# Hedgehog attention beside a SwiGLU block: Q and K logits taken relative to the last feature of each head

## The chip, the cores and the metric

The kernel runs on one core of one Trainium2 chip. The metric is the time of one execution on the device in microseconds (us); the kernel before takes 266.25 us, the median of three runs (266.11 to 266.27). The profile is one such execution (266.31 us), of which the trace shows 265.1 us from the first instruction to the last. The core has a matrix engine (PE, TensorE, with its weight loads shown apart as PEld), a vector engine (DVE), an activation engine (ACT), GpSimd (POOL), and a queue (SP) that issues most of the transfers. All of them run beside each other and wait for one another through semaphores.

## The reference

The input is normalised once (`xn`), and two branches work on it: a linear attention with 32 heads of 20 features, and a gated MLP. Their sum is added to `x`. Cut to what matters:

```python
# S = 2048 rows, D = 640, H = 32 heads, Dh = 20, F = 1536, all bf16
q, k, v = split_heads(xn @ wqkv)
pq = jnp.einsum("bhsd,hdf->bhsf", q, w_phi)          # logits, 20 per head
pk = jnp.einsum("bhsd,hdf->bhsf", k, w_phi)
phi_q = concat([softmax(pq), softmax(-pq)], axis=-1)  # 40 features per head
phi_k = concat([softmax(pk), softmax(-pk)], axis=-1)
kv  = jnp.einsum("bhsf,bhsd->bhfd", phi_k, v)
z   = jnp.einsum("bhsf->bhf", phi_k)
num = jnp.einsum("bhqf,bhfd->bhqd", phi_q, kv)
den = jnp.einsum("bhqf,bhf->bhq", phi_q, z)[..., None] + 1e-6
attn = merge_heads(num / den) @ wo
mlp  = (silu(xn @ w1) * (xn @ w3)) @ w2
out  = x + attn + mlp
```

## The kernel before

The per-head matrices `w_phi` are multiplied into the Q and K columns of `wqkv` once, at the start (`fold_mm`: the folding), so that one matmul gives the logits straight from `xn`. The folded K weights lie beside the V weights in `WVK`, the folded Q weights in `Wqp`.

```python
def fold_mm(which, dc, k):              # 5 calls for K (which=1), 5 for Q (which=0)
    ...                                 # 6 or so narrow matmuls into two PSUM banks
    dst = Wqp[:, dc, :] if which == 0 else WVK[:, dc, D:2 * D]
    evac(dst..., bank2(k, 320))         # 640 columns, PSUM -> bf16, on ACT or DVE

def k_exps(t, c):                       # t: one of 16 tiles of 128 rows
    o = ekt[:, t, :].rearrange("p (h s f) -> p h s f", s=2, f=DH)
    i = PS[:, c:c + D].rearrange("p (h f) -> p h f", f=DH)
    for sg in range(2):                 # exp(x) and exp(-x)
        act(o[:, :, sg, :], i, ACT.Exp, 1.0 if sg == 0 else -1.0)

def k_features(t, k):                   # tiles 0 to 3 (their V was made before)
    for q, lo, hi in ((0, 0, 512), (1, 512, D)):
        for i in range(DC):             # DC = 5 slices of the 640 inputs
            mm(bank(k + q, hi - lo), xnT[:, i, t * 128:(t + 1) * 128], WVK[:, i, D + lo:D + hi], ...)
    k_exps(t, 512 * k)

def vk_features(t, k):                  # tiles 4 to 15: V and K in one go
    for q, lo, hi in ((0, 0, 512), (1, 512, 1024), (2, 1024, 2 * D)):
        for i in range(DC):
            mm(bank(k + q, hi - lo), xnT[:, i, ...], WVK[:, i, lo:hi], ...)
    act(v2c[:, t, :, 1:61], ..., ACT.Copy)
    k_exps(t, 512 * k + D)

def q_features(t, k):
    for q, lo, hi in ((0, 0, 18), (1, 18, 32)):        # heads
        n = DH * (hi - lo)                              # 360 and 280 columns
        for i in range(DC):
            mm(bank(k + q, n), xnT[:, i, ...], Wqp[:, i, DH * lo:DH * hi], ...)
        ...                                             # exp(x), exp(-x) on ACT into eqt

def normalise(e, c, n):                 # softmax's division, the same for Q and K
    tensor_reduce (DVE): sum over the 20 features of each of the 64 (66) groups
    reciprocal (DVE)
    tensor_tensor x2 (POOL): e = e * reciprocal, two halves of a tile
```

The K features of all 16 tiles are multiplied with V in `kv_sum`. A tile of Q features goes through a transposing transfer (`EqT`) and then `q_tok` multiplies it with the result of `kv_sum`; the quotient is transposed again into `oT`. The MLP is 48 units of ten 128x512 matmuls (`mlp`), which stand in no order with the attention, and the output matmuls end the kernel.

No engine has a hand-written order. A planner in the kernel holds a list of streams (norms, folding, attention, queries, MLP units, outputs and so on), estimates when each next piece could start, and puts the earliest one next; what comes out is one fixed list of instructions for each engine. MLP units thereby fill the places where the attention has to wait. `PACE0` and `PACE` say how many MLP units are to lie between two tiles of queries.

```python
def paced(t):
    left = NB * FC - 2 - pace[0]
    return PACE0 * t if t < 4 else PACE0 * 4 + min(PACE, (left - PACE0 * 4) / 12) * (t - 4)
```

Of the kernel before, what the change touches and what calls it, by code (L numbers as in the profile page):

```python
# [3 lines left out]
ACT = mybir.ActivationFunctionType  # L4
ALU = mybir.AluOpType
# [4 lines left out]
D = 640  # L10
H = 32
DH = 20
F = 1536
T = S // 128
DC = D // 128
FC = F // 128
NB = S // 512
# [10 lines left out]
def heads_of_chunk(c):  # L28
    return (128 * c) // DH, (128 * c + 127) // DH

# [215 lines left out]
def bass_parallel_sum__linear_kernel_hedgehog__glu_gated_swiglu__prompt_kernel(  # L246
# [11 lines left out]
    bf = DT.bfloat16  # L258
# [2 lines left out]
    LEAD = 5  # L261
    AHEAD = 0
    PACE = 2.6
    PACE0 = 2.6
    f32 = DT.float32
    P = _Program(nc)

# [5 lines left out]
    def region(size):  # L273
        o = top[0]
        top[0] = o + (size + 31) // 32 * 32
        assert top[0] <= arena_size, top[0]
        return a0 + o

    def new(name, shape, dtype, offset=None):
        size = mybir.dt.size(dtype)  # L280
        for n in shape[1:]:
            size *= n
        return P.sbuf(name, shape, dtype, region(size) if offset is None else offset)

    ident = new("ident", [128, 128], bf)
    GM = new("GM", [128, DC, H], bf)
    phi_s = new("phi_s", [128, DC, DH], bf)
    BDc = new("BDc", [128, DC, 8 * DH], bf)
    bst = new("bst", [128, T, 16], f32)
# [9 lines left out]
    xnT = new("xnT", [128, DC, S], bf)  # L299
    w1_s = new("w1_s", [128, DC, F], bf)  # L300
    w3_s = new("w3_s", [128, DC, F], bf)
    Wqp = new("Wqp", [128, DC, D], bf)
    th = new("th", [128, 3, 512], f32)
    RT = region(3072)
    t1 = new("t1", [128, 3, 512], bf, RT)
# [1 line left out]
    RR = region(4 * D * 2)  # L307
    xres = new("xres", [128, 4, D], bf, RR)
    xT1 = new("xT1", [128, DC, 512], bf, RR)

    RX = region(20480)
    x_tok = new("x_tok", [128, T, D], bf, RX)
    hT2 = new("hT2", [128, FC, 512], bf, RX)
    wo_s = new("wo_s", [128, DC, D], bf, RX + 12288)

    RKV = region(12800)
    WVK = new("WVK", [128, DC, 2 * D], bf, RKV)
    EqT0 = new("EqT0", [128, QC, 512], bf, RKV)
    xT2 = new("xT2", [128, DC, 512], bf, RKV)
    xT = {0: xT1, 1: xT1, 2: xT2}  # L320
# [6 lines left out]
    ekt = new("ekt", [128, T, 2 * D], bf, RE)  # L327
# [14 lines left out]
    eqt = new("eqt", [128, 3, QC * 128], bf, RW + 1408)  # L342
# [3 lines left out]
    PS = nc.alloc_psum_tensor("PS", [128, 8 * 512], f32)  # L346
# [3 lines left out]
    def bank(k, cols=512, off=0, rows=128):  # L350
        return PS[0:rows, k * 512 + off:k * 512 + off + cols]

    def bank2(k, cols):
        return PS[:, k * 512:(k + 2) * 512].rearrange("p (b c) -> p b c", c=512)[:, :, 0:cols]


    def mm(o, l, r, start, stop, shared=False, cost=None):
        n = free(r)
        P.op("PE", "matmul", [o], [l, r], (o, l, r),
             dict(start=start, stop=stop, skip_group_check=shared),  # L360
             cost=n / 2400 + 0.0027 if cost is None else cost)
# [11 lines left out]
    def act(o, i, f, scale=1.0):  # L373
        P.op("ACT", "activation", [o], [i], (o, i, f), dict(scale=scale),
             cost=0.17 + free(o) / 1200)

    def tt(eng, o, a, b, f, fast=1):
        c = 0.16 + free(o) / 960 / fast if eng == "DVE" else 0.2 + free(o) * 1.7 / 1000
        P.op(eng, "tensor_tensor", [o], [a, b], (o, a, b, f), cost=c)
# [5 lines left out]
    def copy(eng, o, i, fast=1):  # L385
        if eng == "ACT":
            act(o, i, ACT.Copy)
        else:
            P.op(eng, "tensor_copy", [o], [i], (o, i), cost=0.14 + free(o) / 960 / fast)

    def evac(o, i):

        a = P.free["ACT"] + 0.17 + free(o) / 1200
        d = P.free["DVE"] + 0.14 + free(o) / 960 / (2 if i.dtype == bf else 1)
        copy("ACT" if a <= d else "DVE", o, i, 2 if i.dtype == bf else 1)

    def memset(eng, o, v):
        P.op(eng, "memset", [o], [], (o, v), cost=0.15 + free(o) / 960)
# [138 lines left out]
    def fold_mm(which, dc, k):  # L537
        first = [True, True]
        for e in range(DC):
            h0, h1 = heads_of_chunk(e)  # L540
            lo, hi = DH * h0, DH * (h1 + 1)
            for q in range(2):
                a, b = max(lo, 320 * q), min(hi, 320 * q + 320)
                if a < b:
                    mm(bank(k + q, b - a, a - 320 * q), wqkT[:, which * DC + e, 128 * dc:128 * dc + 128],
                       BDc[:, e, a - lo:b - lo], first[q], e == DC - 1 or (q == 0 and e == 2), True)
                    first[q] = False
        dst = Wqp[:, dc, :] if which == 0 else WVK[:, dc, D:2 * D]
        evac(dst.rearrange("p (b c) -> p b c", c=320), bank2(k, 320))


    VH = (0, 300, D)

# [30 lines left out]

    def k_exps(t, c):
        o = ekt[:, t, :].rearrange("p (h s f) -> p h s f", s=2, f=DH)
        i = PS[:, c:c + D].rearrange("p (h f) -> p h f", f=DH)
        for sg in range(2):
            act(o[:, :, sg, :], i, ACT.Exp, 1.0 if sg == 0 else -1.0)

    def k_features(t, k):
        for q, lo, hi in ((0, 0, 512), (1, 512, D)):
            for i in range(DC):
                mm(bank(k + q, hi - lo), xnT[:, i, t * 128:(t + 1) * 128], WVK[:, i, D + lo:D + hi],
                   i == 0, i == DC - 1)
        k_exps(t, 512 * k)

    def vk_features(t, k):
        for q, lo, hi in ((0, 0, 512), (1, 512, 1024), (2, 1024, 2 * D)):
            for i in range(DC):  # L600
                mm(bank(k + q, hi - lo), xnT[:, i, t * 128:(t + 1) * 128], WVK[:, i, lo:hi], i == 0, i == DC - 1)
        act(v2c[:, t, :, 1:61], PS[:, 512 * k:512 * k + 660].rearrange("p (c n) -> p c n", n=60), ACT.Copy)
        k_exps(t, 512 * k + D)

    def q_features(t, k):
        if t < 3:
            e = eqt[:, t, :].rearrange("p (c r) -> p c r", r=128)
            memset("DVE", e[:, :, 120:128], 1.0)
            memset("DVE", e[:, QC - 1, 80:120], 1.0)
        for q, lo, hi in ((0, 0, 18), (1, 18, 32)):  # L610
            n = DH * (hi - lo)
            for i in range(DC):
                mm(bank(k + q, n), xnT[:, i, t * 128:(t + 1) * 128], Wqp[:, i, DH * lo:DH * hi],
                   i == 0, i == DC - 1)
            e = eqt[:, t % 3, :].rearrange("p (c r) -> p c r", r=128)[:, :, 0:120]
            e = e.rearrange("p c (h s f) -> p c h s f", s=2, f=DH)
            for sg in range(2):
                x = 1.0 if sg == 0 else -1.0
                if q == 0:
                    act(e[:, 0:6, :, sg, :], bank(k, n).rearrange("p (c h f) -> p c h f", h=3, f=DH), ACT.Exp, x)  # L620
                else:
                    act(e[:, 6:10, :, sg, :],
                        bank(k + 1, 240).rearrange("p (c h f) -> p c h f", h=3, f=DH), ACT.Exp, x)
                    act(e[:, 10, 0:2, sg, :], bank(k + 1, 40, 240).rearrange("p (h f) -> p h f", f=DH), ACT.Exp, x)

    nnorm, held = [0], {}

# [127 lines left out]
    def norms():  # L755
        yield lambda: (memset("DVE", zero[:], 0.0), memset("DVE", warm[:], 0.0), first_loads(), consts())
        yield lambda: act_sums(1)
        yield lambda: ln_stats(0, 1)
        yield lambda: act_mean(1)
        yield lambda: ln_apply(0, 0, 256)  # L760
        done["first"] = 1
        yield lambda: act_rstd(1)
        yield lambda: ln_apply(0, 256, D)
        done["first"], done["ln"] = 2, 1
        while done["t0"] < 2:
            yield None
        yield lambda: ln_sums(2, 0)
        yield lambda: ln_apply(1)
        done["ln"] = 2
        yield lambda: (ln_sums(2, 1), ln_rstd(2, 1))  # L770
        yield lambda: ln_sums(3, 0)
        yield lambda: ln_apply(2)
        done["ln"] = 3
        yield lambda: (ln_sums(3, 1), ln_rstd(3, 1))
        yield lambda: ln_apply(3)
        done["ln"] = 4
        yield block_diag
        todo = []
        for t in range(4, T + 2, 2):
            if t == T or t > done["k"] + LEAD or t == 12 and done["t"] < 8:  # L780
                for u in todo:
                    yield lambda u=u: ln_apply(u)
                    done["ln"] = u + 1
                todo = []
            if t == T:
                break
            while t > done["k"] + LEAD or t == 12 and done["t"] < 8:
                yield None
            yield lambda t=t: ln_stats(t, 2)
            for u in todo:  # L790
                yield lambda u=u: ln_apply(u)
                done["ln"] = u + 1
            todo = [t, t + 1]
        yield consts_late
# [185 lines left out]
    n = len(streams)  # L980
    heads, alive = [None] * n, [True] * n
    while any(alive):
# [34 lines left out]
        i, ops, after = best[2:]  # L1017
# [48 lines left out]
```

The softmax here doesn't subtract the row's maximum and nothing guards it: scores larger than these inputs give would overflow.

## Time and profile before

| what | before |
|---|---|
| time, median of 3 | 266.25 us |
| span of the trace | 265.1 us |
| PE busy | 260.4 us, 1716 instructions seen |
| DVE busy | 183.0 us |
| ACT busy | 106.9 us |
| POOL busy | 94.4 us |
| granted PE clock | 1.00 throughout |

The page gives the busy time of each engine, then the span in 40 slices with the share that each engine worked, then the chain of work that ended last, and then groups of instructions of one kind with their number, total and mean duration, and the idle time before them. In this kernel every instruction is issued through one helper, so the line number (L104) is the same everywhere and the names of the tiles tell the groups apart: `ekt` are the K features, `eqt` the Q features, `hT` and `t` belong to the MLP, `WVK` and `Wqp` are weights, `PS` is PSUM. Durations of single matmuls overlap (a matmul of 512 columns shows 379 ns while the next one starts after some 216 ns), so the pace of PE is read from the starts of neighbouring groups and not from the mean duration. A few per cent of the matmul records are missing: the program has 1744.

### The profile page before, as it was taken

The page shows a single profiled execution, that of the slowest core. Times are in us where ns is not written, and L with a number is a line of the kernel's source. Part 1 is how long each engine was busy: PE and PEld are TensorE (multiplying, and loading weights), DVE is VectorE, ACT ScalarE, POOL GpSimd, SP SyncE. Part 2 cuts the span into 40 slices and gives each one's busy share as a digit, 9 for nine tenths or more (in the row PEclk, how much of TensorE's full clock was granted, in tenths as well). Part 3 has the DMA queues.
Part 4 walks back from the last instruction along what each step waited for, and adds up shares of the span by engine and source line. Part 5 has one row for each costly group of instructions (what it writes and reads, how often), then busy time and mean ns, then how long its engine had stood idle before and what let it go on. Part 6 is the DMA issues. An engine that isn't in the chain of part 4 may idle for free.

```text
span 265.1 us, 4353 instructions
## 1 busy us (share of the span) xinstructions
PE 260.4 (98%) x1716; PEld 141.0 (53%) x1744; DVE 183.0 (69%) x319; ACT 106.9 (40%) x228; POOL 94.4 (36%) x107
## 2 busy tenths in 40 slices
PE   8999999999999999999999999999999999999997
PEld 4655545565558555555545455555544444444773
DVE  4668999999796679989995979897986103221112
ACT  5656988799870445355225245445220000000000
POOL 4311587989995033333330704333420000000000
DMA  7996068923302890445614174366292362461431
GB/s 221 289 315 170 4 157 236 179 52 53 120 2 56 256 213 11 88 73 99 113 27 80 37 123 80 72 123 121 52 110 49 78 149 74 99 198 22 104 124 52
DMA packets 76757, 29.68 MB, mean 112 GB/s; under 512 B 65472, under 2 KB 76736, under 8 KB 76736
## 3 DMA queue, kind: packets, MB, share of 16 engines
q1 hardware_dynamic: 76592, 29.23, 49.3%
q8 instruction: 14, 0.23, 0.4%
q10 hardware_dynamic: 144, 0.16, 0.2%
q14 instruction: 7, 0.06, 0.1%
HBM read 10.84 MB, written 2.62 MB: 51 GB/s over the span
## 4 chain that ended last, share of the span: by engine, by line
PE 95%; DVE 2%; DMA 1%; issue 1%; POOL 0%
PE PS L104 95%; DMA x_tok<-in_A_x_dram 1%; DVE t L104 1%; DVE hT L104 0%; DVE bst L104 0%; POOL rstd L104 0%; DVE mv L104 0%; DVE x_tok L104 0%; DVE xres L104 0%
## 5 line engine op out<-in xcount | busy, mean ns | idle before, releaser
L104 PE MATMUL PS<-xnT,w_s 128*128 128x512 bf16 x464 | 105.5, 379 | 0.9 <-issue 0.2
L104 PEld LDWEIGHTS PS<-xnT,w_s 128*128 128x128 bf16 x480 | 46.2, 98 | 51.4 <-DVE xnT L104 0.3
L104 POOL TENSOR_TENSOR eqt<-eqt,rS 128x600 bf16<-128x600 bf16 (+1 forms) x32 | 41.1, 1305 | 72.4 <-DVE rS L104 72.4
L104 ACT ACTIVATE th<-PS 128x512 f32<-128x512 f32 x48 | 28.6, 596 | 50.7 <-PE PS L104 50.6
L104 PE MATMUL PS<-WVK,xnT 128*128 128x512 bf16 (+4 forms) x255 | 45.1, 329 | 0.3
L104 POOL TENSOR_TENSOR ekt<-ekt,rS 128x640 bf16<-128x640 bf16 x32 | 39.8, 1275 | 4.9 <-DVE rS L104 4.9
L104 DVE SCALAR_TENSOR_TENSOR t<-th,PS 128x512 bf16<-128x512 f32 x48 | 32.0, 668 | 13.7 <-ACT th L104 13.5
L104 PE MATMUL PS<-hT,w_s 128*128 128x512 bf16 x179 | 41.1, 379 | 0.0
L104 ACT ACTIVATE eqt<-PS 128x240 bf16<-128x240 f32 (+1 forms) x96 | 27.2, 348 | 27.7 <-PE PS L104 25.9
L104 PEld LDWEIGHTS PS<-WVK,xnT 128*128 128x128 bf16 x260 | 24.2, 98 | 19.3 <-ACT WVK L104 0.4
L104 DVE SCALAR_TENSOR_TENSOR hT<-t,PS 128x512 bf16<-128x512 bf16 x48 | 33.0, 687 | 1.6
L104 DVE TENSOR_TENSOR xT<-PS,xT 128x512 bf16<-128x512 f32 x15 | 10.1, 685 | 34.7 <-PE PS L104 31.6
L104 PEld LDWEIGHTS PS<-hT,w_s 128*128 128x128 bf16 x180 | 17.6, 98 | 21.3
L104 DVE TENSOR_REDUCE S<-eqt 128x66 f32<-128x1320 bf16 x16 | 24.2, 1514 | 1.4 <-ACT eqt L104 1.4
L104 DVE TENSOR_REDUCE S<-ekt 128x64 f32<-128x1280 bf16 x16 | 23.3, 1455 | 2.2 <-ACT ekt L104 2.2
L104 PE MATMUL PS<-Wqp,xnT 128*128 128x360 bf16 (+1 forms) x160 | 24.3, 299 | 0.1
L104 ACT ACTIVATE ekt<-PS 128x640 bf16<-128x640 f32 x32 | 22.3, 702 | 1.3 <-PE PS L104 0.8
L104 PEld LDWEIGHTS PS<-Wqp,xnT 128*128 128x128 bf16 x160 | 15.1, 98 | 7.1
L104 DVE RECIPROCAL rS<-S 128x64 f32<-128x64 f32 (+1 forms) x32 | 17.9, 560 | 1.1
L104 PE MATMUL PS<-oT,wo_s 128*128 128x512 bf16 x70 | 17.9, 379 | 0.3
L104 DVE TENSOR_TENSOR o_tok<-PS,g_s 128x360 bf16<-128x360 f32 (+1 forms) x32 | 15.7, 491 | 1.1
L104 DVE BATCH_NORM_STATS2 bst<-x_tok 128x6 f32<-128x320 bf16 x30 | 13.9, 481 | 2.8 <-DMA x_tok<-in_A_x_dram 2.4
(55 smaller groups left out, 153.7 us busy)
## 6 DMA issues: line engine op xcount, KB each, us to landing
w_s<-in_B_w_dram SPq DMA_DIRECT2D x6, 640.0 KB, 6.3
x_tok<-in_A_x_dram SPq DMA_DIRECT2D x3, 640.0 KB, 5.2
w_s<-in_B_w_dram SPq DMA_DIRECT2D x1, 1920.0 KB, 8.0
out_dram<-ot SPq DMA_DIRECT2D x3, 640.0 KB, 3.5
wo_s<-in_A_wo_dram SPq DMA_DIRECT2D x1, 800.0 KB, 5.0
WVK<-in_A_wqkv_dram SPq DMA_DIRECT2D x2, 320.0 KB, 3.8
xres<-in_A_x_dram SPq DMA_DIRECT2D x1, 640.0 KB, 4.8
x_tok<-in_A_x_dram SPq DMA_DIRECT2D x3, 160.0 KB, 3.3
```

Source lines behind the costliest of these rows:

```text
L104: o = _Op(eng, lambda: m(*args, **kw), r, w, cost)
```

## The change

Softmax doesn't change when the same number is taken from all logits of a head. The change takes the logit of the last feature from all 20, so that the last one is always zero and its exponential always one, for softmax(x) and softmax(-x) alike. This is done in the folded weights: from the 20 columns of a head the last is subtracted, and only 19 are kept. Thus a tile has 608 columns of logits for Q and for K in place of 640, the exponentials of the last feature are not computed, and the ones are written by a fill (`memset`). Sums, division and everything behind them work on 20 features as before.

It is meant to shorten the Q and K matmuls and the exponentials by a twentieth. For it, the folding gets a second step: ACT copies the folded columns to SBUF in float32, and POOL subtracts and writes bf16. `PACE0` goes from 2.6 to 3.2.

```diff
+FD = DH - 1
+KD = H * FD
-    PACE0 = 2.6
+    PACE0 = 3.2
+    FQ = "POOL"
-    Wqp = new("Wqp", [128, DC, D], bf)
+    Wqp = new("Wqp", [128, DC, KD], bf)
+    fold = new("fold", [128, 2, D], f32, RR)
-    WVK = new("WVK", [128, DC, 2 * D], bf, RKV)
+    WVK = new("WVK", [128, DC, D + KD], bf, RKV)
 ... fold_mm
-        dst = Wqp[:, dc, :] if which == 0 else WVK[:, dc, D:2 * D]
-        evac(dst.rearrange("p (b c) -> p b c", c=320), bank2(k, 320))
+        dst = Wqp[:, dc, :] if which == 0 else WVK[:, dc, D:D + KD]
+        w = fold[:, dc % 2, :]
+        copy("ACT", w.rearrange("p (b c) -> p b c", c=320), bank2(k, 320))
+        w = w.rearrange("p (h f) -> p h f", f=DH)
+        tt("POOL" if which else FQ, dst.rearrange("p (h f) -> p h f", f=FD), w[:, :, 0:FD],
+           w[:, :, FD].unsqueeze(2).to_broadcast([128, H, FD]), ALU.subtract)
 ... k_exps
-            act(o[:, :, sg, :], i, ACT.Exp, 1.0 if sg == 0 else -1.0)
+            act(o[:, :, sg, 0:FD], i, ACT.Exp, 1.0 if sg == 0 else -1.0)
 ... k_features, vk_features
-        for q, lo, hi in ((0, 0, 512), (1, 512, D)):
+        for q, lo, hi in ((0, 0, 512), (1, 512, KD)):
-        for q, lo, hi in ((0, 0, 512), (1, 512, 1024), (2, 1024, 2 * D)):
+        for q, lo, hi in ((0, 0, 512), (1, 512, 1024), (2, 1024, D + KD)):
 ... q_features (the exponentials likewise, on 19 of 20 places)
-            n = DH * (hi - lo)
+            n = FD * (hi - lo)
+        e = eqt[:, t % 3, :].rearrange("p (c r) -> p c r", r=128)[:, :, 0:120]
+        memset("POOL", e.rearrange("p c (n f) -> p c n f", f=DH)[:, :, :, FD], 1.0)
 ... norms, after block_diag
+        yield lambda: memset("POOL", ekt[:].rearrange("p t (n f) -> p t n f", f=DH)[:, :, :, FD], 1.0)
```

More of the change, by code (lines that the diff above doesn't have):

```diff
@@ L314, in bass_parallel_sum__linear_kernel_hedgehog__glu_gated_swiglu__prompt_kernel @@
     wo_s = new("wo_s", [128, DC, D], bf, RX + 12288)
-    RKV = region(12800)
-    WVK = new("WVK", [128, DC, 2 * D], bf, RKV)
+    RKV = region(12480)
+    WVK = new("WVK", [128, DC, D + KD], bf, RKV)
     EqT0 = new("EqT0", [128, QC, 512], bf, RKV)
@@ L586, in k_exps @@
         o = ekt[:, t, :].rearrange("p (h s f) -> p h s f", s=2, f=DH)
-        i = PS[:, c:c + D].rearrange("p (h f) -> p h f", f=DH)
+        i = PS[:, c:c + KD].rearrange("p (h f) -> p h f", f=FD)
         for sg in range(2):
-            act(o[:, :, sg, :], i, ACT.Exp, 1.0 if sg == 0 else -1.0)
+            act(o[:, :, sg, 0:FD], i, ACT.Exp, 1.0 if sg == 0 else -1.0)
     def k_features(t, k):
-        for q, lo, hi in ((0, 0, 512), (1, 512, D)):
+        for q, lo, hi in ((0, 0, 512), (1, 512, KD)):
             for i in range(DC):
@@ L610, in q_features @@
         for q, lo, hi in ((0, 0, 18), (1, 18, 32)):
-            n = DH * (hi - lo)
+            n = FD * (hi - lo)
             for i in range(DC):
-                mm(bank(k + q, n), xnT[:, i, t * 128:(t + 1) * 128], Wqp[:, i, DH * lo:DH * hi],
+                mm(bank(k + q, n), xnT[:, i, t * 128:(t + 1) * 128], Wqp[:, i, FD * lo:FD * hi],
                    i == 0, i == DC - 1)
@@ L619, in q_features @@
                 if q == 0:
-                    act(e[:, 0:6, :, sg, :], bank(k, n).rearrange("p (c h f) -> p c h f", h=3, f=DH), ACT.Exp, x)
+                    act(e[:, 0:6, :, sg, 0:FD], bank(k, n).rearrange("p (c h f) -> p c h f", h=3, f=FD), ACT.Exp, x)
                 else:
-                    act(e[:, 6:10, :, sg, :],
-                        bank(k + 1, 240).rearrange("p (c h f) -> p c h f", h=3, f=DH), ACT.Exp, x)
-                    act(e[:, 10, 0:2, sg, :], bank(k + 1, 40, 240).rearrange("p (h f) -> p h f", f=DH), ACT.Exp, x)
+                    act(e[:, 6:10, :, sg, 0:FD],
+                        bank(k + 1, 12 * FD).rearrange("p (c h f) -> p c h f", h=3, f=FD), ACT.Exp, x)
+                    act(e[:, 10, 0:2, sg, 0:FD],
+                        bank(k + 1, 2 * FD, 12 * FD).rearrange("p (h f) -> p h f", f=FD), ACT.Exp, x)
+        e = eqt[:, t % 3, :].rearrange("p (c r) -> p c r", r=128)[:, :, 0:120]
+        memset("POOL", e.rearrange("p c (n f) -> p c n f", f=DH)[:, :, :, FD], 1.0)
     nnorm, held = [0], {}
```

## The prediction

> **What bounds the kernel now.** I read the page from the top: busy time of each engine first, then the chain that ended last.
>
> ```profile
> PE 260.4 (98%) x1716; PEld 141.0 (53%) x1744; DVE 183.0 (69%) x319; ACT 106.9 (40%) x228; POOL 94.4 (36%) x107
> PE 95%; DVE 2%; DMA 1%; issue 1%; POOL 0%
> ```
>
> PE is busy 98% of the span and makes up 95% of the chain. A busy PE need not be a PE at its pace, so I asked next who PE waited for. The waits of PE itself are all of this:
>
> ```profile
> PE PS L104 <- PEq L1051: 0.8, 1, 0.8
> PE PS L104 <- DVE x_tok L104: 0.3, 1, 0.3
> PE PS L104 <- issue: 0.2, 1, 0.2
> ```
>
> That is 1.3 us in 265 (the last number of a line is its longest wait), and the first 0.8 us is the start. To see the pace, I took from the timeline the starts of the output chunks, each 17 matmuls of 512 columns (the counts fall short where records are missing):
>
> ```profile
> 204.22 1.24 PE L104 MATMUL PS<-oT,wo_s 128*128 128x512 bf16 x4
> ...
> 207.89 1.24 PE L104 MATMUL PS<-oT,wo_s 128*128 128x512 bf16 x5
> ...
> 211.56 1.24 PE L104 MATMUL PS<-oT,wo_s 128*128 128x512 bf16 x5
> ```
>
> One chunk takes 3.67 us, so a matmul 3.67 / 17 = 215.9 ns. The chunks of 34 matmuls with 320 columns start at 244.59 and 249.20: 4.61 / 34 = 135.6 ns. The difference, 80.3 ns for 192 columns, is 0.418 ns a column, and 2 ns a matmul are left. Even the 176 narrow matmuls of kv_sum (61 columns or fewer) pass between 81.40 and 86.41, 28.5 ns each. So time is proportional to columns plus 2 to 3 ns a matmul, with no floor above 28.5 ns that a new shape would meet.
>
> The check that matters: I added up all matmuls of the planned order, at columns / 2400 us plus 3 ns, from the first transpose at 6.2 us. The sum puts kv_sum at 81.28 (trace: 81.40) and the last matmul at 263.19; the trace has the last DVE addition waiting for it at 263.26. **PE runs without a gap from 6.2 us to the end.** Whatever is taken from PE shortens the kernel, unless it leaves a gap; whatever is added elsewhere costs only if PE then waits.
>
> The second thing to see is where another engine is close to being the bound. The table by stretches of 10 us (columns: length, then PE, PEld, DVE, ACT, POOL busy, PE clock, DMA share, GB/s) shows it:
>
> ```profile
> 30.00:40.00 10.00, 9.95 (x53) 4.97 (x53) 9.73 (x20) 8.76 (x13) 8.12 (x9) 1.00 0.48 111
> ...
> 60.00:70.00 10.00, 9.95 (x65) 5.55 (x65) 8.55 (x11) 9.10 (x15) 9.63 (x9) 1.00 0.43 115
> 70.00:80.00 10.00, 9.90 (x55) 5.37 (x55) 8.44 (x12) 6.86 (x15) 9.86 (x12) 1.00 0.01 2
> 80.00:90.00 10.00, 9.95 (x206) 7.62 (x205) 5.34 (x14) 2.84 (x8) 3.11 (x3) 1.00 0.44 101
> ```
>
> Between 30 and 80 us, while the K features are made, DVE and then POOL are nearly full; after 80 us POOL has much time. The last POOL work on K ends at 80.58, and kv_sum, which needs it, starts at 81.40. The plan before has well under 1 us to spare there.
>
> **What the Trainium skill says.** "TensorE: Matmul & The Clock Gate", section "Wait — 56ns, not 53.3ns?", gives columns / 2.4 GHz plus about 2.5 ns from start to start for a warm array, and about 25 ns at the least. The trace agrees: 215.9 ns at 512 columns, 28.5 ns at 61, clock 1.00. "ScalarE: Activation LUTs", section "What ACT_TABLE_LOAD costs", gives 0.833 ns an element; the exponentials here, 702 ns for 640 and 368 ns for 240, give 0.835. "GPSIMD Engine Reference", section 3.1, has a float32 tensor_tensor of 2048 elements at 4497 ns, 2.2 ns an element; here bf16 with a float32 factor follows 0.18 us + 1.71 ns an element (1202 ns at 600, 1407 at 720). The new subtraction reads float32 from both sides, which no instruction of this size here does. No page bears on a fill of scattered bf16 elements on POOL.
>
> **The change part by part.**
>
> *Removed from PE.* K: 16 tiles x 5 slices x 32 columns = 2560 columns. Q: 16 x 5 x (18 + 14) = 2560. The number of matmuls stays 1744. 5120 columns x 0.417 ns = **2.13 us**, all on the path. The narrowest new shape, 96 columns where there were 128, still takes some 43 ns, above the 28.5 ns seen. The same sum over the new planned order ends at 261.06 in place of 263.19.
>
> *Removed from ACT.* 32 elements of each of 32 K exponentials and 64 elements a tile of 16 Q tiles: 2048 x 0.835 ns = 1.7 us, beside other work, worth nothing by itself. Two layernorm applications move from ACT to DVE in the new order (0.9 us less on ACT, 0.56 us more on DVE, each), and one evacuation of 0.82 us the other way.
>
> *Added to POOL.* Rows of the profile to size it:
>
> ```profile
> L104 POOL TENSOR_TENSOR ekt<-ekt,rS 128x640 bf16<-128x640 bf16 x32 | 39.8, 1275 | 4.9 <-DVE rS L104 4.9
> L104 POOL MEMSET v<- 128x176 bf16 x1 | 0.9, 885 | 0.0
> ```
>
> Ten subtractions of 608 elements: by the bf16 line above 0.18 + 608 x 1.71 ns = 1.22 us each, 12.2 us; by the skill's float32 rate 1.4 us or so, an estimate. The fill of one place in twenty of ekt is 1024 elements; the one scattered bf16 fill here takes 885 ns for 176, about 4.5 ns each above 0.1 us, so some 4.7 us at worst. Sixteen fills of 66 elements: 0.4 us each, 6.3 us. Together 23 us, POOL to about 117 us. All lies beside PE; the question is only whether PE waits for it. Three places:
>
> (a) *First K features.* They need the five subtracted slices of WVK. The fill of ekt lies in a hole of POOL (idle from 14.06 to 20.66), so it should cost nothing. Subtractions 1 and 2 run after rstd, from 21.96; 3, 4 and 5 follow the copies on ACT and end near 25.6, 26.8 and 28.1 at 1.22 us each. The plan puts one more MLP unit (2.16 us) ahead of the K features, which now start at 27.35 by my sum and need slice 5 at 28.2. That is a margin of 0.1 us; at 1.44 us a subtraction, PE waits about 1 us. I count 0.3 us.
>
> (b) *kv_sum.* In the new plan the last K tile leaves PE at 81.0. Then 0.7 us V copy, 1.4 us exponentials, 2.05 us sum and reciprocal, 2.5 us POOL: 87.8 with latencies. kv_sum starts at 88.8 and needs the last tile at 89.2. POOL's backlog (32 x 1.235 + 5 x 1.22 + rstd and fills, from 32.3) is met by an MLP pause between K tiles 9 and 10. Margin about 1.4 us, expected cost near zero.
>
> (c) *Queries.* From the end of a tile's Q matmuls to its q_tok the old plan leaves 12.5 us at the least, the new one 11.6 for one tile and 13.1 or more for the others. The chain needs about 2 (exponentials) + 0.4 (the new fill, which waits for them and holds the sum) + 2.1 (sum, reciprocal) + 2.6 (POOL) + 3.6 (median landing of the transfer) = 10.7 us plus queueing. One tile may wait some tenths; I count 0.15 us.
>
> *Sum:* 266.25 - 2.13 + 0.3 + 0.15 = **264.6 us**.
>
> **The rivals.** First, *POOL becomes the bound in the K stage*. For it: POOL at 9.86 of 10 us before kv_sum, and five subtractions of 6.1 us added right there. Against it: kv_sum itself is moved from 81.3 to 88.8 with MLP units taken from later, and total PE work doesn't grow. If POOL fell behind by 3 us, the time would be 266 to 267. Second, *the wait for the folded weights takes the place of what was won*: a longer float32 subtraction would be paid nearly three times over at (a); 1 us puts the time at 265.3. Third, *DVE becomes the bound*: it was at 9.7 of 10 us from 30 to 60 without making PE wait, and gets only 0.3 us more in all; but the order of MLP units and K tiles is new, and a PSUM bank freed late stops PE at once. That costs tenths. Fourth, *nothing is won because the narrow matmuls meet a floor*: 28.5 ns at 61 columns speaks against it.
>
> **Range and chances.** The gain can't exceed 2.13 us by this mechanism, so 264.1 is the floor but for noise of 0.1. Each us lost is a us above. I give 264.6 with 264.0 to 266.0. 2% is 5.3 us, more than twice what can be won; a loss of that size needs PE gaps of 7.5 us. Faster by over 2%: 0.01; within 2%: 0.97; slower: 0.02.
>
> **What would show it.** PE busy should fall by about 2 us, to 258.3, and the span to some 263.4. The Q matmuls should be 342 and 266 columns and no slower than that; a wait of PE for POOL at WVK near 28 us shows (a) and the duration of the subtraction; kv_sum near 88.8 or later shows (b); PE gaps before the KVc matmuls, with the EqT transfer as releaser, show (c). POOL should show about 117 us. The prediction is wrong if PE has gaps of more than 2 us anywhere after 10 us, or if columns prove not to be what PE's time follows.

## The result and the profile after

The changed kernel takes 264.01 us (median of six runs, 263.87 to 264.20) where the kernel before takes 266.25. The ratio is 0.9917, with a 95% interval of 0.9904 to 0.9930. That is 2.24 us less.

The first two views of the page after, the busy times and the chain that ended last:

```profile
PE 257.5 (98%) x1716; PEld 140.1 (53%) x1744; DVE 182.1 (69%) x319; ACT 105.5 (40%) x228; POOL 116.5 (44%) x134
PE 87%; DVE 5%; POOL 3%; issue 2%; ACT 1%; DMA 1%
```

PE's busy time went down by 2.9 us and POOL's up by 22 us. (A PE busy time is good to about 1 us only, since its ends are modelled: a second trace of the changed kernel, after_again, shows 258.5.) PE's share of the chain fell from 95% to 87%, which looks as if the Q features on POOL had become a part of the bound. They have not; the waits of PE itself (total, times, longest) say so:

```profile
PE PS L106 <- PEq L1062: 0.8, 1, 0.8
PE PS L106 <- DVE x_tok L106: 0.6, 1, 0.6
PE PS L106 <- issue: 0.2, 1, 0.2
```

All three lie in the start, before 12 us. The chain takes detours over work that ended at nearly the same time as PE needed it, and a detour isn't a wait. The table by stretches (length, then PE, PEld, DVE, ACT, POOL busy, PE clock, DMA share, GB/s) shows PE full where POOL is fullest:

```profile
60.00:70.00 10.00, 9.95 (x68) 5.87 (x69) 9.62 (x12) 7.35 (x12) 9.86 (x12) 1.00 0.43 115
70.00:80.00 10.00, 9.89 (x56) 5.19 (x57) 5.32 (x7) 6.40 (x10) 10.00 (x10) 1.00 0.01 2
80.00:90.00 10.00, 9.95 (x99) 5.99 (x99) 8.10 (x13) 5.12 (x12) 8.78 (x8) 1.00 0.00 0
```

The rows of the costlier new or changed groups, from the groups of instructions with shapes kept apart (busy time, mean ns of one, idle time before):

```profile
L106 PE MATMUL PS<-Wqp,xnT 128*128 128x342 bf16 x80 | 14.2, 307 | 0.0
L106 PE MATMUL PS<-WVK,xnT 128*128 128x96 bf16 x20 | 1.5, 206 | 0.0
L106 POOL TENSOR_TENSOR WVK<-fold 128x608 bf16<-128x608 f32 x5 | 5.9, 1201 | 0.1
L106 POOL MEMSET ekt<- 128x1024 bf16 x1 | 4.6, 4607 | 0.0
L106 POOL MEMSET eqt<- 128x66 bf16 x16 | 6.3, 391 | 18.1 <-ACT eqt L106 18.1
```

The sum that carried the prediction, columns / 2400 us plus 3 ns a matmul over the planned order, can now be held against the trace of the changed kernel. With its start set at 6.0 us it puts the first Q matmuls at 83.0, kv_sum at 88.6, the eighth KVc group (the 11 matmuls of `q_tok` for one tile of queries) at 153.0 and the last one at 205.2. The trace has 82.9, 88.5, 152.9 and 205.1. PE has no gap here either. From the second group of transposes to the last group of matmuls PE takes 256.21 us before (6.18 to 262.39) and 254.02 us after (5.85 to 259.87), 2.19 us less; the start of that stretch moves by some tenths from run to run.

### The profile page after: what moved, and what is told of

The parts are those of the page before. It is cut to its first block, busy times and chain, and to the rows that moved or that the text cites. A ratio compares the mean times of both kernels' runs of the same rounds, so it can differ in the third digit from the quotient of the medians.

```text
span 262.6 us, 4391 instructions
## 1 busy us (share of the span) xinstructions
PE 257.5 (98%) x1716; PEld 140.1 (53%) x1744; DVE 182.1 (69%) x319; ACT 105.5 (40%) x228; POOL 116.5 (44%) x134
## 4 chain that ended last, share of the span: by engine, by line
PE 87%; DVE 5%; POOL 3%; issue 2%; ACT 1%; DMA 1%
PE PS L106 87%; POOL eqt L106 3%; DVE S L106 2%; ACT eqt L106 1%; DMA x_tok<-in_A_x_dram 1%; DVE t L106 1%; DVE bst L106 1%; DVE rS L106 0%; DVE hT L106 0%; DVE x_tok L106 0%; POOL rstd L106 0%; DVE o_tok L106 0%; DVE mv L106 0%; DVE g_s L106 0%; DVE xres L106 0%
## 5 line engine op out<-in xcount | busy, mean ns | idle before, releaser
L106 PE MATMUL PS<-WVK,xnT 128*128 128x512 bf16 (+4 forms) x256 | 43.9, 325 | 0.2
L106 ACT ACTIVATE eqt<-PS 128x228 bf16<-128x228 f32 (+1 forms) x96 | 26.5, 345 | 22.8 <-PE PS L106 20.3
L106 PE MATMUL PS<-Wqp,xnT 128*128 128x342 bf16 (+1 forms) x160 | 23.1, 292 | 0.0
L106 ACT ACTIVATE ekt<-PS 128x608 bf16<-128x608 f32 x32 | 22.1, 696 | 2.3 <-PE PS L106 1.8
```

Of the source, the lines that this page charges most:

```text
L106: o = _Op(eng, lambda: m(*args, **kw), r, w, cost)
```

## The experiments

All runs are compared with runs of the kernel before on the same chip: 266.17 us beside k_only, q_only, cols_back and eighteen, 266.16 beside sub_twice, pace_old and fill_dve, 266.22 beside before_pace, rel_phi and after_again, 266.28 beside eighteen_b and ekt_fill_dve.

**K alone (k_only).** Q keeps its 20 columns and its old path.

```diff
-    Wqp = new("Wqp", [128, DC, KD], bf)
+    Wqp = new("Wqp", [128, DC, D], bf)
 ... fold_mm: for which == 0 the evacuation of before
 ... q_features: as before
```

> 19 columns per head for K alone; Q as before with 20. Theory (PE has no gaps, its time follows the columns): 2560 columns fewer, 1.07 us less than before, 265.2. Rival (the extra POOL work ahead of K and kv_sum costs something that the Q half pays back): 265.7 or more. Rival (the Q half alone brings the gain, since the third K matmul is narrow): 266.2.

Measured: 264.93 us (264.86 to 265.00), 1.24 less than before; ratio 0.9947, interval 0.9930 to 0.9964.

**Q alone (q_only).** The mirror image: K keeps 20 columns.

> 19 columns per head for Q alone; K as before with 20. Theory: 2560 columns fewer, 1.07 us less than before, 265.2, and together with the K half the whole gain of 2.2. Rival (the new fill in the chain of each Q tile makes PE wait): 265.7 or more, with gaps before the KVc matmuls.

Measured: 265.09 us (265.01 to 265.18), 1.08 less; ratio 0.9953, interval 0.9938 to 0.9968. The halves add up to 2.32 us against 2.24 for the whole. Each half brings what its 2560 columns are worth, 1.07 us, within some 0.2, and neither costs anything that the other pays back.

**The columns put back (cols_back).** Everything that the change adds stays, and only the matmuls are 640 wide again.

```diff
-        for q, lo, hi in ((0, 0, 512), (1, 512, KD)):
+        for q, lo, hi in ((0, 0, 512), (1, 512, D)):
-            n = FD * (hi - lo)
+            n = DH * (hi - lo)
 ... the weights 640 wide with a last column of zeros per head; exponentials read 19 of 20
```

> As the changed kernel in everything (subtraction, fills, exponentials of 19 features, PACE0 3.2), but the weights keep all 20 columns per head and the matmuls are 640 wide again, the last column being zero and unread. Theory (only the columns count): the time of before, 266.2 within 0.2, with POOL at 117 us busy. Rival (the shorter exponentials on ACT or the new PACE0 bring part of the gain): 265.5 or less. Rival (the added POOL work costs a part that the columns hid): 266.7 or more.

Measured: 266.06 us; ratio 0.9994, interval 0.9987 to 1.0000. The first line of its page:

```profile
PE 259.8 (98%) x1715; PEld 140.7 (53%) x1744; DVE 184.2 (70%) x320; ACT 105.1 (40%) x227; POOL 117.6 (44%) x134
```

POOL is as busy as in the changed kernel and 23 us busier than before, and the time is that of before but for 0.1 us. PE waits for nothing in this trace but at the start (1.3 us in all, as before). So the added POOL work costs PE nothing, the shorter exponentials bring nothing, and the gain is that of the columns.

**The K subtractions done twice (sub_twice).** This takes away the room at the place that the prediction called (a), with PE's order unchanged.

```diff
+            for _ in range(2):
+                P.op("POOL", "tensor_tensor", [o], [a, b], (o, a, b, ALU.subtract), cost=0.60)
```

> The changed kernel, with each of the five subtractions of the K weights on POOL done twice, while the planner is told half the cost, so that PE's order stays the same. The slices are ready at about 24.0, 26.4, 28.8, 31.2 and 33.5 us, and PE needs them at 27.5 to 28.3. Theory (PE has no slack after the start, every wait adds in full): a PE gap of about 5.2 us near 28 us and a time of 269.2. Rival (the MLP work or later slack takes the delay up): 264 to 266.

Measured: 271.93 us (271.25 to 272.56); ratio 1.0217, interval 1.0199 to 1.0236. That is 7.9 us above the changed kernel where 5.2 were expected. The waits of PE give the gap itself:

```profile
PE PS L106 <- POOL WVK L106: 4.9, 3, 2.0
```

They are three waits, with single matmuls between them:

```profile
29.12 0.39 PE L106 MATMUL PS<-WVK,xnT 128*128 128x512 bf16 x1 [1.04 <-POOL WVK L106]
31.56 0.61 PE L106 MATMUL PS<-WVK,xnT 128*128 128x512 bf16 x1 [2.05 <-POOL WVK L106]
34.00 5.25 PE L106 MATMUL PS<-WVK,xnT 128*128 128x512 bf16 x26 [1.83 <-POOL WVK L106]
```

The rest is in the clock column (the last but two) of the stretches around it:

```profile
25.00:30.00 5.00, 3.47 (x20) 1.24 (x16) 1.38 (x2) 2.03 (x4) 4.84 (x5) 1.00 0.17 33
30.00:35.00 5.00, 1.61 (x8) 0.78 (x9) 3.42 (x8) 0.35 (x1) 4.72 (x6) 0.64 0.01 2
35.00:40.00 5.00, 5.00 (x26) 2.29 (x24) 3.00 (x3) 3.48 (x6) 1.55 (x4) 0.68 0.01 3
40.00:45.00 5.00, 5.00 (x29) 2.40 (x28) 4.86 (x11) 4.61 (x7) 4.74 (x6) 1.00 0.34 67
```

From the first K matmul to the MLP unit behind the first three K tiles PE takes 3.66 us in the changed kernel (27.45 to 31.11) and 11.60 us here (27.48 to 39.08): 7.94 more, of which 4.9 are waits. The other 3.0 go for the most part to the lower clock until PE had been busy for a while: where PE is busy throughout, from 35 to 40, a clock of 0.68 is 1.6 us of them by itself. "TensorE: Matmul & The Clock Gate" of the Trainium skill, section "What's actually happening", describes the mechanism: the clock is halved after an idle window of about 3.4 us and comes back after a busy one. Here no single wait was that long; three of 1.0 to 2.1 us with single matmuls between them were enough. The whole 7.9 us reach the end of the kernel. No later stage gives any of it back, which is what a PE without gaps means.

**The old PACE0 (pace_old).**

```diff
-    PACE0 = 3.2
+    PACE0 = 2.6
```

> The changed kernel with PACE0 at 2.6 as before. Theory (order doesn't matter as long as PE has no gap): 264.0 within 0.2. Rival (the new PACE0 is needed, because kv_sum or the first Q tiles come too early for POOL): 264.5 or more, with PE waiting near 80 to 90 us.

Measured: 264.28 us (264.22 to 264.68); ratio 0.9934, interval 0.9917 to 0.9950. Its trace follows its planned sum until a KVc group planned for 123.4, which starts at 123.9, and stays 0.3 to 0.5 us late from there on. The waits of PE name it:

```profile
PE PS L106 <- ACT eqt L106: 0.2, 1, 0.2
```

So the order may matter a little: 0.27 us by the medians, just outside the 0.2 that I had allowed, at the edge of what these runs tell apart, and not where the rival put it.

**The new PACE0 in the kernel before (before_pace).**

> The kernel before with PACE0 at 3.2, nothing else. Theory: PE has no gap in either order, 266.25 within 0.15. Rival (a part of the gain comes from the order that PACE0 gives): 265.9 or less.

Measured: 266.41 us; ratio 1.0015, interval 1.0004 to 1.0026. PACE0 alone brings nothing; if anything it costs 0.2 us (266.22 beside it). It suits the changed kernel, and is no part of the gain.

**The fill of the Q tiles on DVE (fill_dve).**

```diff
-        memset("POOL", e.rearrange(...)[:, :, :, FD], 1.0)
+        memset("DVE", e.rearrange(...)[:, :, :, FD], 1.0)
```

> The changed kernel with the fill of each Q tile on DVE in place of POOL. In the changed kernel the Q tiles follow each other in a ring of POOL fill, DVE sum, reciprocal and POOL division that takes 5.14 us a turn. Theory: the ring shortens to about 4.8 us, POOL's busy time falls by 6.3 us to 110, and the time stays at 264.0 within 0.2, since PE has no gaps to close. Rival (the ring holds PE back somewhere): 263.7 or less.

Measured: 264.10 us (263.92 to 264.42); ratio 0.9925, interval 0.9910 to 0.9939. The ring that this was to shorten shows in the POOL timeline of the changed kernel. Each division on POOL is followed by the fill for the next tile, which stands behind it in POOL's queue, and DVE's sum for that tile waits for the fill:

```profile
127.38 2.57 POOL L106 TENSOR_TENSOR eqt<-eqt,rS 128x600 bf16<-128x600 bf16 x2 [2.24 <-DVE rS L106]
129.89 0.39 POOL L106 MEMSET eqt<- 128x66 bf16 x1
132.52 2.57 POOL L106 TENSOR_TENSOR eqt<-eqt,rS 128x600 bf16<-128x600 bf16 x2 [2.24 <-DVE rS L106]
```

A turn is 5.14 us. With the fill on DVE a turn can take 4.17 us (139.26 to 143.43) or less, POOL comes down to 110.8 us busy, and the time stays. The ring has to deliver 16 tiles in the 110 us or so that the plan gives them (the first Q matmuls start at 82.9, the last division at 195.3), and at 5.14 us it needs 82.

**18 columns (eighteen).** This asks whether the gain goes on with the columns. Feature 18's logit is left out and its exponential set to one, so this kernel computes less than the reference.

```diff
-FD = DH - 1
+FD = DH - 2
+        memset("DVE", e.rearrange(...)[:, :, :, FD + 1], 1.0)      # in q_features
+        yield lambda: memset("DVE", ekt[:].rearrange(...)[:, :, :, FD + 1], 1.0)
```

> 18 columns per head kept in place of 19, for Q and K; the logit of feature 18 is left out and its exponential set to one, so the result isn't the reference's. The second column of ones is filled on DVE. Theory (0.417 ns a column with no floor down to 64 columns): another 5120 columns, another 2.13 us less, 261.9, twice the gain of the change. Rival (a floor for narrow matmuls, or DVE and POOL catching up with a shorter PE): 262.5 or more.

Measured: 271.18 us (270.92 to 272.53); ratio 1.0192, interval 1.0163 to 1.0221: slower than before. Most of the loss is not in the columns but in the large fill that I had put on DVE: PE starts the first K features at 33.8 where the planned sum has 27.2. DVE's timeline:

```profile
15.79 0.20 DVE L106 CAST v<-PS 128x40 bf16<-128x40 f32 x1 [0.85 <-ACT v L106]
22.39 0.91 DVE L106 MEMSET ekt<- 128x1024 bf16 x1 [6.40 <-issue]
22.94 0.88 DVE L106 SCALAR_TENSOR_TENSOR t<-th,PS 128x512 bf16<-128x512 f32 x1
```

DVE stands for 6.4 us. The planner makes this fill wait for the POOL fill that writes its neighbours, which ends at 18.69; PE then lacks PSUM banks that DVE should have emptied, and its clock drops as in sub_twice (0.78 and 0.88 between 25 and 35 us). Smaller PE waits follow, among them 0.8 us for ACT after the sixth folding and, in the Q tiles, 0.5 us for ACT and 0.6 us for a transposing transfer.

**18 columns, one fill (eighteen_b).** Both places of a group are one aligned word of 4 bytes, so one POOL fill writes both, and no engine gets an instruction more than in the changed kernel.

```diff
+        yield lambda: memset("POOL", ekt[:].bitcast(f32)....[:, :, :, DH // 2 - 1], TWO_ONES)
```

> 18 columns per head again (the logit of feature 18 is left out, its exponential set to one), but both places are filled by one POOL fill of 4-byte words, so that no engine gets an instruction that the changed kernel lacks. In the run eighteen the second fill, on DVE, waited for the first on POOL from 16.0 to 22.4 us and held up DVE, ACT and PE behind it. Theory: with that wait gone PE has no gap of over 0.5 us, and the time is 261.9 within 0.3, twice the gain of the change. Rival (18 columns themselves do harm, by a floor for narrow matmuls or by DVE and POOL falling behind): 263 or more.

Measured: 263.33 us (263.21 to 263.46); ratio 0.9894, interval 0.9877 to 0.9910. Faster than the changed kernel, but by 0.68 us and not by 2.13: my expectation failed, and the time is in the rival's range. The planned sum against the trace shows where. They agree until the sixth folding (planned 56.2, started 56.2); the next one is 1.0 us late (59.1, 60.1), the one after the next 1.4 (67.1, 68.4), and about as much remains to the end. The weight loads, which wait first, name the reason:

```profile
PEld PS L107 <- ACT fold L107: 1.0, 1, 1.0
PEld PS L107 <- ACT ekt L107: 0.5, 1, 0.5
PEld PS L107 <- ACT v L107: 0.3, 1, 0.3
```

PE waits for PSUM banks that ACT has not yet emptied. These waits, and not a floor, take 1.3 to 1.4 us of the 2.13 that the columns are worth again. The changed kernel has none of them: there an MLP unit stands between the sixth folding and the next tile (at 57.17), where this kernel goes straight on to the tile. Why the plan has no MLP unit there was not tried. DVE, which empties the MLP's banks, is at 9.8 of 10 us from 30 to 60, but it is at 9.6 to 9.8 in the changed kernel too.

**The K fill on DVE (ekt_fill_dve).** The changed kernel with this one fill moved, to learn what held DVE in the run eighteen.

> The changed kernel with the fill of the K features on DVE in place of POOL, so that it has no POOL fill to wait for. If the wait of DVE in the run eighteen was one for the end of the POOL fill, the DVE fill starts at once here, near 16 us, takes 0.9 us, and the time stays at 264.0 within 0.3. If the DVE fill itself was slow, it holds DVE up for 6 us again and the time is 270 or more.

Measured: 265.84 us; ratio 0.9984, interval 0.9977 to 0.9991. Neither expectation fits in its number; the cause of the second does, a slow fill, with 4 us and not 6. DVE's timeline:

```profile
13.92 0.69 DVE L106 SCALAR_TENSOR_TENSOR hT<-t,PS 128x512 bf16<-128x512 bf16 x1
18.20 0.91 DVE L106 MEMSET ekt<- 128x1024 bf16 x1 [3.59 <-PE PS L106]
18.74 0.89 DVE L106 SCALAR_TENSOR_TENSOR t<-th,PS 128x512 bf16<-128x512 f32 x1
```

In the program this fill waits for nothing, yet DVE stands from 14.61 to 18.74. The next DVE work had its input ready at 16.69, when the tanh on ACT (`th`) ended, and POOL stood idle from 14.09 to 22.54, so neither was what held DVE. I take it that the record of 0.91 us is only the tail of the fill, and that the fill holds DVE for about 4.1 us. In the run eighteen the same holds: from the end of the POOL fill at 18.69 to the next DVE work at 22.94 are 4.25 us, and the wait for POOL was the other part. The 4.1 us delay everything behind them in DVE's queue and cost PE waits of 0.5, 0.4 and 0.4 us, for ACT, POOL and DVE in turn (its weight loads, which wait first, 0.7, 0.9 and 0.5 us). The time lost against the changed kernel is 1.8 us.

**The last column taken off w_phi (rel_phi).** If only PE's columns count, the folding itself can have fewer.

```diff
+        tt("POOL", phr[:], phi_s[:, :, 0:FD], phi_s[:, :, FD]...to_broadcast([128, DC, FD]), ALU.subtract)
-               phi_s[:, c, :].unsqueeze(1).to_broadcast([128, n, DH]),
+               phr[:, c, :].unsqueeze(1).to_broadcast([128, n, FD]),
 ... fold_mm, 304 columns a bank
-        copy("ACT", w..., bank2(k, 320))
-        tt("POOL" if which else FQ, dst..., w[:, :, 0:FD], w[:, :, FD]..., ALU.subtract)
+        evac(dst.rearrange("p (b c) -> p b c", c=HB), bank2(k, HB))
```

> The same 19 columns, but the last column is taken off w_phi itself (100 elements a partition, once on POOL) before the block-diagonal matrices are made; the folding matmuls are then 133 and 76 columns wide in place of 140 and 80, their result goes straight from PSUM to bf16 weights as before the change, and the float32 copy and the ten subtractions of 608 elements are gone. Theory (only PE's columns count): 360 columns fewer, 0.15 us less than the changed kernel, 263.85; POOL's busy time falls by 11.5 us to 105. Rival (the removed POOL work was costing time in the K stage): 263.5 or less. Rival (the two POOL steps ahead of the first folding delay PE): 264.2 or more, with a gap near 17 us.

and the changed kernel beside it (after_again):

> The changed kernel once more, beside rel_phi: 264.0 within 0.2.

Measured: 263.90 us (263.80 to 264.00), ratio 0.9913, interval 0.9900 to 0.9926; the changed kernel 264.02 us (263.86 to 264.21), ratio 0.9918, interval 0.9905 to 0.9931. The difference of the medians is 0.12 us of 0.15 expected, and the intervals overlap, so it isn't established. What is: without the ten subtractions and the float32 copy, at 105.6 us of POOL in place of 116.7, the kernel is at least as fast, with less in it.

## Why the prediction was right

**The mechanism and the main term held.** 2.13 us for 5120 columns against 2.24 measured. The two halves, 1.24 and 1.08, and cols_back, 0.1 us below before, show that it is the columns and nothing else. The missing 0.1 is the size of the scatter between runs: PE's own stretch, from the second group of transposes to the last matmuls, shrank by 2.19 us in one trace of the changed kernel and by 2.04 in the other.

**The two allowances were the miss.** I added 0.3 us at (a) and 0.15 us at (c); both came out as zero, which is the 0.6 us between 264.6 and 264.0, together with the scatter. They pushed the forecast up, so that 264.01 lies only just above the lower end of the range, 264.0; that it is still inside owes something to luck. At (a) the subtraction took 1.20 us, as the bf16 line had said (1.22), and not the 1.4 us that I had estimated from the skill's float32 rate ("GPSIMD Engine Reference", section 3.1). The five didn't have to wait for the copies on ACT as I had reckoned, but ran back to back from 21.61, so that the last ended at 27.6 and not at 28.1; PE needed it at 28.3. That lateness at this place is paid in full was right: sub_twice made it a wait of 4.9 us. At (c) no KVc group was late.

**Margin (b) was misread.** I reckoned POOL's last K division to end at 87.8. It ended at 88.47, because the last three tiles stood in line on POOL and came through back to back from 81.06; POOL was busy for 21.98 of the 22 us from 66 to 88:

```profile
81.06 7.41 POOL L106 TENSOR_TENSOR ekt<-ekt,rS 128x640 bf16<-128x640 bf16 x6
88.50 5.16 PE L106 MATMUL PS<-v,ekt 128*128 128x61 bf16 x176
```

The pause between K tiles 9 and 10 met most of POOL's backlog and not all of it. But I had also set the need for that last division too early. A tile is divided in two halves, and kv_sum goes through the features in chunks of 120, each over all 16 tiles. Its 16th matmul, at about 88.9, reads only the first half of the last tile, which was ready at 87.2; the second half is first read by the 96th matmul, at about 91.3. So the margin was about 1.7 us, somewhat more than the 1.4 that I gave, and the plan before had some 2.5 us there (first half at 79.3, needed at 81.8) and not "well under 1 us".

**POOL's load was well sized.** Fills of 4.6 and 0.39 us (4.7 and 0.4 predicted), 116.5 us busy (117).

**The saving on ACT was not.** I put it at 1.7 us by 0.835 ns an element. The trace shows, before and after, for the K exponentials:

```profile
L104 ACT ACTIVATE ekt<-PS 128x640 bf16<-128x640 f32 x32 | 22.3, 702 | 1.3 <-PE PS L104 0.8
```

```profile
L106 ACT ACTIVATE ekt<-PS 128x608 bf16<-128x608 f32 x32 | 22.1, 696 | 2.3 <-PE PS L106 1.8
```

That is 6 ns in place of 27, and with the Q exponentials 0.4 us in all. It lay beside PE, so nothing came of it. And one layernorm application moved from ACT to DVE, not two.

**The rivals.** POOL as the bound: full before kv_sum, but with 1.7 us to spare. The folded weights as a new wait: only when doubled. DVE as the bound: not with 19 columns; at 18 the waits named are for ACT, and a part of DVE in them is not shown. A floor for narrow matmuls: none seen at 96 columns, nor at 64 in eighteen_b, whose trace follows its sum wherever PE isn't waiting.

## What to carry to other kernels

Where one engine runs without gaps, sum its work by the pace between starts, lay the sum over the planned order, and compare it with the trace at a few landmarks. An agreement to a tenth of a us says more than any busy share, and the first landmark that is late says where to look. Work moved to engines with room is then free, but only until one of them is late for the engine without gaps; that lateness is paid in full, and more than in full when PE's clock drops. A gain that goes with the columns need not go on with more of them: here the next step of the same size brought a third.

## What the hardware showed that was not expected

- *Scattered fills of 2 bytes are slow on both engines.* One bf16 in every 20 costs 4.5 ns an element on POOL (4607 ns for 1024). On DVE it is about 4.0 ns (4.1 us for 1024, worked out from how long DVE stood). "VectorE: DVE Perf Modes" of the Trainium skill, section "Zero memsets can be issued as uint32 (trn2)", gives a memset one cycle an element whatever the type; the measurement for this pattern is some four times that. Filled as aligned words of 4 bytes, the same number of places takes POOL 1.9 ns each, as the groups of eighteen_b show:

```profile
L107 POOL MEMSET ekt<- 128x1024 f32 x1 | 1.9, 1927 | 0.0
L107 POOL MEMSET eqt<- 128x66 f32 x16 | 3.5, 216 | 23.7 <-ACT eqt L107 22.3 <-DVE g_s L107 1.4
```

- *The record of such a DVE fill seems to be only its tail*: 0.91 us where DVE stood for 4.1. The idle time ahead of it, put down to "issue" or to PE, then belongs to the fill.
- *Rows of 19 cost ACT almost what rows of 20 do.* The K exponentials take 702 ns for 32 rows of 20, 696 for rows of 19 and 655 for rows of 18. All are bf16 rows placed at every 40 bytes; whether the odd length is the cause wasn't tried.
- *Gaps of 1 to 2 us in a row lower PE's clock*, to 0.64 and 0.68 over the 10 us from 30 to 40, so that gaps of 4.9 us in all cost 7.9.
